# Re-dealing PSUM banks, an earlier store, a ninth buffer and a one-row load in an fp32 attention and mixer kernel

## The chip, the cores and the metric

One core of one Trainium2 chip. The time is the device's time of one execution in microseconds (us), and lower is better. A result is the median of several executions. The profiled execution counts a span that is about 1.8 us shorter than the time; places within the kernel are given on the clock of that span.

## The reference

Two blocks follow each other. The first is a decaying linear attention over 4 x 8 heads, 768 positions and 64 columns, in blocks. The second is a mixer on its output x (4 x 768 x 512): a low-rank mixing along the sequence, and a two-layer product with 2048 hidden columns. Cut to what matters:

```python
Dmask = np.where(rel >= 0, lam[:, None, None] ** rel[None, :, :], 0.0)   # decays, one lam per head
for b in range(nb):                                    # blocks of the sequence
    intra = einsum(einsum(qb, kb) * Dmask, vb)
    inter = einsum(qb * lam_pow, kv_state)
    out[:, :, sl] = intra + inter
    kv_state = lam_block * kv_state + einsum(kb * rev_pow, vb)
x = out.transpose(0, 2, 1, 3).reshape(B, S, H * D)
u = x + (x.transpose(0, 2, 1) @ U @ V).transpose(0, 2, 1)
return u + np.maximum(u @ w_ch1, 0.0) @ w_ch2
```

## The kernel before

Attention goes in 24 steps, one tile of 128 positions in each. Seven steps behind, a tile is mixed (`mix`, giving u) and transposed for the first product (`turn`). Then comes the "head": units of first-product matmuls; among the first three the last mixings and transposes are woven. The rest of the kernel is matmuls back to back. The 8 banks of PSUM are dealt by tag: a ring of four named "bank", and two pairs "pz" and "pd".

```python
x_pool = mix_ctx.enter_context(tc.tile_pool(name="x", bufs=8, side="right"))
consts = att_ctx.enter_context(tc.tile_pool(name="consts", bufs=1))
raw_pool = att_ctx.enter_context(tc.tile_pool(name="raw", bufs=3))     # q, k, v land here
...
def bank(shape, name, tag="bank"):
    return ps.tile(shape, FP32, tag=tag, bufs={"bank": 4}.get(tag, 2), name=name)
lamb = consts.tile([P, H], FP32, name="lamb")
...
# scores: pss -> "pz"; outputs: px -> "pd"; state: pkv -> "pd"
# pq, pk, pxn, pp, pr, pu, put -> "bank"
...
def back(s):
    ...
    xs[s] = x_pool.tile([P, C], FP32, tag="x", name="x_nat")
    nc.scalar.copy(xs[s].rearrange("p (c n) -> p c n", n=P), px)     # copy of x, ScalarE
...
def mix(s):
    pu = bank([P, C], "pu")
    nc.tensor.matmul(out=pu, lhsT=v_hl[:, c * P : (c + 1) * P], rhs=p_hl, start=True, stop=True)
    nc.vector.tensor_tensor(out=xs[s], in0=pu, in1=xs[s], op=ALU.add)   # x becomes u, VectorE
...
def turn(s):
    pt = bank([P, CT, P], "put")
    ...                                            # four transposes of u into put
    if g >= FG:
        ...                                        # ends with uf, ScalarE's copy of put
        nc.sync.dma_start(out=u_d[s], in_=xs.pop(s))
        return
    ...
    def rest():                                    # run in the next step
        ...
        nc.sync.dma_start(out=u_d[s], in_=xs.pop(s))
...
nc.scalar.dma_start(out=lamb, in_=lam.unsqueeze(0).broadcast_to([P, H]))
for name, engine in (("q", nc.sync), ("k", nc.scalar), ("q", nc.sync), ("k", nc.sync), ("v", nc.scalar)):
    load_next(name, engine)
```

In the head and after it, `banks(n, other)` takes pz and pd of a unit from ("bank", "bank") or ("pz", "pd"), in turn.

## Time and profile before

| | before |
|---|---|
| time, median of 3 | 702.17 us (701.72 to 702.33) |
| span of the profiled execution | 700.1 us, granted TensorE clock 1.000 |
| attention, to the last mixing product within it | 145.4 us |
| head, to the last transposes of u | 171.7 us |
| matmuls back to back, to the last one | 695.8 us |

TensorE is the engine that sets the end. So a change of buffers is read in one way: which waits of TensorE go, which come, and at which of these four places. Idle time of another engine matters only where TensorE stands behind it.

### The profile page before, as it was taken

The numbers are of one execution on the slowest core, as the hardware profiler recorded it, in microseconds if no ns is written. First come the engines' busy times: TensorE is split into PE (matmuls) and PEld (weight loads), VectorE is DVE, ScalarE is ACT, GpSimd is POOL, SyncE is SP. The second block draws the span as 40 slices with busy tenths as digits, with TensorE's granted clock in tenths as the row PEclk, the third lists the DMA queues.
The fourth block names the chain that finished last, engine by engine and source line by source line (L and its number), as shares of the span: only waits on it lengthen the run. The fifth ranks groups of instructions, "written<-read, shape, count | busy, mean of one in ns | idle before, by whom it ended". The sixth has DMA issues, their size and how long they took to land.

```text
span 700.1 us, 11380 instructions
## 1 busy us (share of the span) xinstructions
PE 683.6 (98%) x4192; PEld 555.9 (79%) x4192; DVE 501.5 (72%) x903; ACT 305.7 (44%) x543; POOL 108.0 (15%) x91
## 2 busy tenths in 40 slices
PE   6999998998999999999999999999999999999997
PEld 5988787976888888888888888888888888888886
DVE  4777776867899777777779525778676586775864
ACT  3776776855456544444445422232232222322320
POOL 3425444533000000000000000012030030300300
PEclk9999999999999999999999999999999999999999
DMA  9997785414577655556567899956344262353431
GB/s 186 223 204 182 170 202 146 120 47 154 195 258 253 223 195 196 201 203 219 208 210 273 279 320 341 356 201 211 92 155 160 90 211 99 116 191 90 166 92 60
DMA packets 131672, 131.18 MB, mean 187 GB/s; under 512 B 81376, under 2 KB 89568, under 8 KB 131616
## 3 DMA queue, kind: packets, MB, share of 16 engines
q1 hardware_dynamic: 129376, 129.92, 59.0%
q10 hardware_dynamic: 2240, 0.53, 0.4%
q8 instruction: 33, 0.54, 0.3%
q14 instruction: 23, 0.19, 0.1%
HBM read 80.09 MB, written 50.33 MB: 186 GB/s over the span
## 4 chain that ended last, share of the span: by engine, by line
PE 91%; DMA 4%; DVE 3%; ACT 1%; issue 0%; ACTq 0%; DVEq 0%
PE pz L634 25%; PE pz L765 13%; PE pz L767 13%; PE pd L769 13%; PE pd L644 13%; PE pss L343 3%; DMA u_d<-x_nat 3%; PE px L366 2%; PE px L361 2%; PE pxn L406 1%; PE pkv L382 1%; PE put L466 1%; PE pq L308 1%; PE pk L308 1%; DMA kraw<-in_k_dram 1%; DVE sm L349 1%
## 5 line engine op out<-in xcount | busy, mean ns | idle before, releaser
L634 PE MATMUL pz<-u_hl,w 128*128 128x512 f32 x768 | 190.4, 398 | 0.0
L634 PEld LDWEIGHTS pz<-u_hl,w 128*128 128x128 f32 x768 | 144.5, 188 | 35.6 <-issue 0.9
L765 PE MATMUL pz<-w_hl,m 128*128 128x512 f32 x384 | 151.6, 396 | 0.0
L767 PE MATMUL pz<-w_hl,m 128*128 128x512 f32 x384 | 151.6, 396 | 0.0
L769 PE MATMUL pd<-w_d,m 128*128 128x512 f32 x384 | 149.9, 396 | 0.0
L748 ACT ACTIVATE m<-mt 128x512 fp32r<-128x512 f32 x96 | 60.7, 632 | 196.3 <-PE pd L769 146.6
L749 DVE SCALAR_TENSOR_TENSOR m<-rm,m 128x512 fp32r<-128x512 f32 x96 | 71.5, 746 | 55.9 <-ACT m L748 55.5
L649 DVE SCALAR_TENSOR_TENSOR r<-pd,r 128x512 f32<-128x512 f32 x96 | 61.8, 686 | 55.5 <-ACT r L640 42.9
L789 POOL TENSOR_TENSOR o<-o,u 128x512 f32<-128x512 f32 x20 | 29.8, 1524 | 450.7 <-DVE o L787 450.7
L644 PE MATMUL pd<-u_d,w 128*128 128x512 f32 x384 | 98.8, 397 | 0.0
L765 PEld LDWEIGHTS pz<-w_hl,m 128*128 128x128 f32 x384 | 72.3, 188 | 17.7
L769 PEld LDWEIGHTS pd<-w_d,m 128*128 128x128 f32 x384 | 72.3, 188 | 17.7
L767 PEld LDWEIGHTS pz<-w_hl,m 128*128 128x128 f32 x384 | 72.3, 188 | 17.6
L644 PEld LDWEIGHTS pd<-u_d,w 128*128 128x128 f32 x384 | 72.2, 188 | 17.4
L640 ACT ACTIVATE r<-pz 128x512 f32<-128x512 f32 x96 | 51.9, 593 | 71.6 <-PE pz L634 71.6
L750 DVE SCALAR_TENSOR_TENSOR m<-m 128x512 fp32r<-128x512 f32 x96 | 69.1, 721 | 0.9
L747 DVE TENSOR_SCALAR mt<-rm 128x512 uint32<-128x512 uint32 x96 | 46.2, 481 | 24.3 <-DMA rm<-r_d 23.7
L349 DVE TENSOR_TENSOR sm<-pss,mask 128x512 f32<-128x512 f32 x48 | 30.9, 686 | 11.4 <-PE pss L343 9.2
L366 PE MATMUL px<-sm,vraw 128*64 128x128 f32 x384 | 35.5, 274 | 0.0
L179 ACT CAST w<-wt 128x512 fp32r<-128x512 f32 x32 | 19.9, 622 | 31.7 <-DVE wt L176 23.5
L361 PE MATMUL px<-qs,kv 128*64 128x128 f32 x320 | 32.1, 279 | 0.0
L136 ACT ACTIVATE sc<-sc,ends 128x512 f32<-128x512 uint32 x29 | 21.0, 723 | 19.1 <-DVE sc L132 19.1
(84 smaller groups left out, 760.7 us busy)
## 6 DMA issues: line engine op xcount, KB each, us to landing
r_d<-r SPq DMA_DIRECT2D x96, 256.0 KB, 2.9
rm<-r_d SPq DMA_DIRECT2D x96, 256.0 KB, 2.6
words<-in_moe_w_ch_dram SPq DMA_DIRECT2D x32, 512.0 KB, 4.4
w_d<-w SPq DMA_DIRECT2D x16, 768.0 KB, 3.3
w_hl<-w_d SPq DMA_DIRECT2D x16, 512.0 KB, 6.4
u_d<-x_nat SPq DMA_DIRECT2D x24, 256.0 KB, 3.7
u<-u_d SPq DMA_DIRECT2D x24, 256.0 KB, 3.9
out_dram<-o SPq DMA_DIRECT2D x24, 256.0 KB, 2.0
```

What stands on the lines that cost most here:

```text
L366: nc.tensor.matmul(out=px[x * D : (x + 1) * D, a, :], lhsT=vr[:, 2 * a + x, :], rhs=sm[:, x, a, :], start=(c == 0), stop=True,)
L634: nc.tensor.matmul(out=acc[g][0], lhsT=w[:, n, ct, :], rhs=uhl[g][:, n, ct, :], start=(ct == 0 and n == 0), stop=(ct == CT - 1 and n == 1),)
L640: nc.scalar.mul(rs[g], acc[g][0], 1.0 + E)
L644: nc.tensor.matmul(out=acc[g][1], lhsT=w[:, 2, ct, :], rhs=ud[g][:, ct, :], start=(ct == 0), stop=(ct == CT - 1),)
L649: nc.vector.scalar_tensor_tensor(rs[g], acc[g][1], 4096.0, rs[g], ALU.mult, ALU.add)
L747: nc.vector.tensor_scalar(t.bitcast(U32), r.bitcast(U32), HI, None, ALU.bitwise_and)
L748: nc.scalar.activation(out=m[:, 0], in_=t, func=AF.Relu)
L749: nc.vector.scalar_tensor_tensor(m[:, 1], r, 0.0, hi, ALU.max, ALU.subtract)
L750: nc.vector.scalar_tensor_tensor(m[:, 2], hi, E, low, ALU.mult, ALU.subtract)
L765: nc.tensor.matmul(out=pz, lhsT=m[:, 0, cols], rhs=hl[:, 0], start=first, stop=False)
L767: nc.tensor.matmul(out=pz, lhsT=m[:, 1, cols], rhs=hl[:, 1], start=False, stop=end)
L769: nc.tensor.matmul(out=pd, lhsT=m[:, 2, cols], rhs=dd, start=first, stop=end)
```

## The change

The intent is fewer waits of TensorE in attention. Instead of four banks in one ring, each tag has two banks: a1 and a2 take the places of "pz" and "pd", and b1 and b2 those of the ring, with pu moved to a2. The store of u is asked for right behind its transposes, x has nine places, and the results of the first product have four buffers for five, to pay for it. The decays come as one row of 32 bytes and are spread over the 128 partitions by a product with ones; before, a broadcast load read the same 32 bytes 128 times.

```diff
-    x_pool = mix_ctx.enter_context(tc.tile_pool(name="x", bufs=8, side="right"))
+    x_pool = mix_ctx.enter_context(tc.tile_pool(name="x", bufs=9, side="right"))
-    def bank(shape, name, tag="bank"):
-        return ps.tile(shape, FP32, tag=tag, bufs={"bank": 4}.get(tag, 2), name=name)
+    def bank(shape, name, tag):
+        return ps.tile(shape, FP32, tag=tag, bufs=2, name=name)
     def constants():
-        make_identity(nc, ident)
-        make_gather()
-                pt = bank([P, n, P], "p" + name)
+                pt = bank([P, n, P], "p" + name, "b2")
-        pss = [bank([P, HP, P], "pss", "pz") for x in range(2)]
+        pss = [bank([P, HP, P], "pss", "a1") for x in range(2)]
-        px = bank([P, HP, P], "px", "pd")
+        px = bank([P, HP, P], "px", "a2")
-            pkv = bank([P, HP, D], "pkv", "pd")
+            pkv = bank([P, HP, D], "pkv", "a2")
-        px = bank([P, CT, P], "pxn")
+        px = bank([P, CT, P], "pxn", "b1")
-        pp = bank([P, C], "pp")
+        pp = bank([P, C], "pp", "a2" if b < B - 1 else "b2")
-        pr = bank([P, C], "pr")
+        pr = bank([P, C], "pr", "b1" if b < B - 1 else "b2")
-        pu = bank([P, C], "pu")
+        pu = bank([P, C], "pu", "a2" if s < NS - NT - 1 else "b2")
-        pt = bank([P, CT, P], "put")
+        pt = bank([P, CT, P], "put", "b1")
         for ct in range(CT):
             ...                                     # the transposes
+        nc.sync.dma_start(out=u_d[s], in_=xs.pop(s))
         ...
-            nc.sync.dma_start(out=u_d[s], in_=xs.pop(s))      # in both places below
-    nc.scalar.dma_start(out=lamb, in_=lam.unsqueeze(0).broadcast_to([P, H]))
+    lam_row = consts.tile([1, H + P], FP32, name="lam_row")
+    nc.scalar.dma_start(out=lam_row[:, 0:H], in_=lam.unsqueeze(0))
+    nc.vector.memset(lam_row[:, H:], 1.0)
     ...                                             # first loads
+    make_identity(nc, ident)
+    make_gather()
+    pl = bank([P, H], "pl", "a2")
+    nc.tensor.matmul(out=pl, lhsT=lam_row[:, H:], rhs=lam_row[:, 0:H], start=True, stop=True)
+    nc.vector.tensor_copy(out=lamb, in_=pl)
-        r_pool = ctx.enter_context(tc.tile_pool(name="r", bufs=5, reuse_waits="tile"))
+        r_pool = ctx.enter_context(tc.tile_pool(name="r", bufs=4, reuse_waits="tile"))
-        tags = ("bank", "bank") if other else ("pz", "pd")
+        tags = ("b1", "b2") if other else ("a1", "a2")
```

More of the change, by code (lines that the diff above doesn't have):

```diff
@@ L488, in rest @@
             nc.gpsimd.tensor_tensor(out=diff, in0=te, in1=low.bitcast(FP32), op=ALU.subtract)
-            nc.sync.dma_start(out=u_d[s], in_=xs.pop(s))
         turned[s] = rest
```

## The prediction

> **What bounds the kernel now.** I read the page first, then the list of waits, then the chain of work in order of time, then the timeline of three stretches. The page says that TensorE is the engine to watch:
>
> ```profile
> PE 683.6 (98%) x4192; PEld 555.9 (79%) x4192; DVE 501.5 (72%) x903; ACT 305.7 (44%) x543; POOL 108.0 (15%) x91
> ```
>
> With 98% busy no change of buffers can be worth 2% unless the 98% hides slack. It does not, in most of the span. The chain from 173 us on is nothing but matmuls of the two mixer products, back to back:
>
> ```profile
> 173.24 3.75 PE pz L634 x16
> 176.99 1.88 PE pd L644 x8
> ```
>
> 3.75/16 is 0.234 us for each 128x512 matmul. The last one starts at 695.8 us, and 522.5 us / 0.2343 us is 2230, as many as I count between those two times (2231 starts). So from 173 us to 696 us TensorE never waits, and nothing in this change makes a matmul shorter. What is left is the first 173 us (attention with the mixing woven in, then the "head", four units of first-product matmuls among which the last transposes of u lie) and 4 us at the end. In the list of waits of the whole span these lines bear on the change:
>
> ```profile
> ACT x_nat L408 <- DMA u_d<-x_nat: 8.6, 5, 3.4
> ...
> PEld pu L449 <- ACT x_nat L408: 5.1, 4, 2.0
> ...
> PE pu L449 <- ACT x_nat L408: 4.0, 3, 1.8
> ...
> DVE mask L270 <- DMA lamb<-in_lam_dram: 2.3, 1, 2.3
> ```
>
> ScalarE's copy of x (L408) needs one of the eight places for x, and stands until the store of an older u has landed; TensorE's pu (L449) then waits for that copy, because in a ring of four banks its bank is the one of the pxn before. Four times, 5.1 us in all: this is what the change is after. The chain shows one of the four in two lines, the store landing and the copy following it:
>
> ```profile
> 59.02 4.85 DMA u_d<-x_nat
> 63.94 0.59 ACT x_nat L408
> ```
>
> **What the Trainium skill says.** "PSUM — Partial Sum Buffer", section "PSUM bank collisions raise a hardware error", has software guard PSUM by bank: a matmul into a bank waits until the last reader of that bank is done. So the grouping of tags decides who waits for whom; the trace agrees, pu waiting 5.1 us for a copy with which it shares nothing but the bank. "Perfetto Trace Analysis", section "Matmul Optimizations", asks that all 8 banks be in use; both kernels use all 8, so the change only re-deals them. "DMA: Bandwidth & Descriptors", section "Anatomy of one DMA — SWDGE (gpsimd) path", gives about 2 us of fixed cost for a transfer issued on that other path; here the 4 KB broadcast of the decays takes 3.7 us from issue to landing, among large loads, so a transfer of one row may land a little earlier but not for nothing.
>
> **The change, part by part.** In the built kernels every engine has its instructions in the same order up to the end of the head, but for the additions below, the place of the store and a few waits.
>
> 1. *Ninth place for x and an earlier store.* Before, u of tile s-8 was stored in step s, just before x of tile s asked for that place. After, u is stored at the end of the step that adds it, and the place is asked for two steps (2 x 5.6 us) later; a store takes 3.7 us (median), 5.5 at most. The wait goes: -5.1 us on TensorE, as in the list of waits. These are all on the path, since TensorE is.
>
> 2. *Decays as a row.* It adds one matmul of 8 columns, a copy of 128x8 and a memset, and takes away 127 of 128 small descriptors. The scans (2.63 us) now start at 4.43 us and end at 7.06, but the first product with the mask is at 10.35, when the scores are there. TensorE starts at 4.78 on q's load and then waits for k's. The new matmul must be over by 4.78, which a landing like today's 4.4 allows. Gain at most the shorter issue ahead of k on the same queue: -0.2 us.
>
> 3. *r with four places.* The r copy (L640) of a unit then waits for the store of two units before. In the trace of before the smallest distance between such a landing and such a copy is 3.1 us: nothing.
>
> 4. *Banks as four uses of two.* In attention a2 now serves pu, px, pkv in turn: three uses a step in two banks, so pkv takes the bank that pu had in the same step, and must wait until VectorE has added it into x (L452). The built kernel shows this: pkv's first matmul waits for VectorE from step 7 on, where it waited for nothing. One step of before:
>
> ```profile
> 52.23 0.48 PE L449 MATMUL pu<-vp 128*128 128x512 f32 x1
> ...
> 53.73 0.69 DVE L452 TENSOR_TENSOR x_nat<-pu,x_nat 128x512 f32<-128x512 f32 x1
> ...
> 54.33 0.60 PEld L382 LDWEIGHTS pkv<-vraw,ks 128*64 128x64 f32 x16
> 54.44 0.64 PE L382 MATMUL pkv<-vraw,ks 128*64 128x64 f32 x16
> ...
> 55.00 0.97 PEld L343 LDWEIGHTS pss<-qt,kt 64*128 64x128 f32 x16
> ```
>
> The add ends at 54.42 and pkv starts at 54.44: by chance no slack at all. A waiting matmul starts about 0.15 us after the add that it needs:
>
> ```profile
> 161.57 0.68 DVE L452 TENSOR_TENSOR x_nat<-pu,x_nat 128x512 f32<-128x512 f32 x1
> ...
> 162.40 0.63 PE L466 MATMUL put<-ident,x_nat 128*128 128x128 f32 x4 [0.40 <-ACT uf L477]
> ```
>
> (the add ends at 162.25; the copy uf named there ends 0.1 us later, but put reads x.) So pkv is put off by 0.13 us a step, and as VectorE's own work of the step hangs on the scores after pkv, the delay comes anew each time. Step by step, end of the add + 0.15 less pkv's start: step 7 (49.47 against 48.85) 0.77; step 13 (85.50, 85.15) 0.50; step 19 (123.68, 123.59) 0.24; step 22 0.21; eight more at 0.13, 1.04: together 2.8 us. In the steps that TensorE waited out before, pkv had 1 us of room, but that room was the wait. At steps 6, 12 and 18 low's product lies between, in the same two banks: pkv then waits for its copy (step 6: copy ends 42.74, pkv's weights load at 42.54, so 0.25 to 0.3), px for the add (0.1 at 12 and 18), put for low_sum's readers (0.14): about 1.2 us. These delays overlap in part with those of steps 13 and 19, so I take 3.6 us for all.
>
> 5. *The same in the head.* Unit 3 is the first to use b1 and b2. Its two pz alternate from the first matmul on, and both are now in b1, where the last two put are. Before, the ring of four gave the second pz the bank of the last put but one, and the last put's bank went to the second pd, 16 matmuls later.
>
> ```profile
> 171.68 0.63 PE L466 MATMUL put<-ident,x_nat 128*128 128x128 f32 x4 [0.77 <-ACT uf L477]
> ...
> 173.08 1.10 PE L634 MATMUL pz<-u_hl,w 128*128 128x512 f32 x4
> ...
> 173.94 0.59 ACT L477 COPY uf<-put 128x512 f32<-128x512 f32 x1 [0.18 <-DVE u_d L474]
> ```
>
> The last reader of the last put ends at 174.53; the second pz would start at 173.31 and now starts at about 174.65: +1.3 us. In the built kernel the second pz of this unit has the same wait for ScalarE as the first. The products after it rotate as before.
>
> The sum: -5.1 - 0.2 + 3.6 + 1.3 = -0.4 us. From 702.17 that is 701.8 us: the change wins one set of waits and buys another.
>
> **Rivals.** (a) The new bank waits cost nothing, as pkv's weights may be loaded in the shadow of px and VectorE gets ahead once the stores are away. Then -5.3 + 1.3, about 698.2. For it: VectorE is idle some 0.7 us a step, before kvc. Against: that idle time lies after the add, waiting for pkv, so it cannot bring the add forward. (b) The new waits feed on each other: with pkv late, kvc, the kv copies and px of the next step are late as well, or the add falls behind its 128x512 neighbours more often; 0.3 us a step more over 14 steps is +4, about 705. For it: VectorE was busy 17.1 of 20 us from 40 to 60 us. Against: px starts 2.6 us after the scores, and kv's copies end about a microsecond before it. (c) The stores still hide behind the loads, since one queue issues all in order and the DMA engines were 76 to 88% busy in this stretch; the x wait would then stay in part, +1 to +3 on my sum, 703 to 705. Against: two whole steps of room.
>
> **Range and chances.** The gain is measured and bounded by 5.3 us; the loss is my estimate from slacks of a few hundredths of a microsecond, good to perhaps 2 us either way. The executions of before lie within 0.6 us. So 699.0 to 704.2 us. Two per cent are 14 us: the stretch that the change touches has less than that to give back (TensorE's idle time is 16 us in all, with start and end), and a loss of 14 us would need a whole new wait of 0.8 us in each step. Faster 0.01, same 0.98, slower 0.01.
>
> **What would show it.** Right: no wait of the x copy for u's store, no wait of pu for the x copy; a new wait of pkv (its weight load) for the add in most steps from 7 on, 2 to 4 us in all; a step in mid attention of about 5.72 us instead of 5.59; a wait of about 1.3 us of pz for uf where unit 3 begins; matmuls at 0.234 us without a gap after that; attention ending about 1.7 us earlier than before. Wrong: if the pkv waits are missing (rival a) or over 5 us (b), if x copies still wait for stores (c), or if any gap opens after 180 us, where I expect none.

## The result, and the profile after

The changed kernel takes 699.0 us (median of 6, 698.76 to 699.32), against 702.01 us (701.16 to 702.33) for the kernel before in the same rounds: a ratio of 0.9959, with 0.9946 to 0.9972 as the 95% interval. Ratios here are the mean time of one kernel's runs over that of the other's of the same rounds, so not quite the ratio of the medians quoted. The span of the profiled execution went from 700.06 to 697.54 us, with the same granted clock (1.000 and 0.999). The change is worth 2.5 to 3 us: within 2%, but 2.8 us better than I had said.

The first view of the kernel after is the row of busy times on its page: engine, busy us, share, number of instructions.

```profile
PE 685.6 (98%) x4194; PEld 556.0 (80%) x4194; DVE 502.0 (72%) x905; ACT 306.6 (44%) x543; POOL 108.0 (15%) x91
```

It answers to the row of before and says almost nothing: two more matmuls, and the same 98%. The differences have to be read from when TensorE reaches the same instruction in both timelines:

| stretch of TensorE | before, us | after, us | difference | predicted |
|---|---|---|---|---|
| start to the scores of step 1 | 13.18 | 11.80 | -1.38 | -0.2 |
| from there to the 18th pu, the last in attention | 132.18 | 130.05 | -2.13 | -5.1 + 3.6 |
| from there to the last put | 26.32 | 25.94 | -0.38 | 0 |
| from there to the last matmul | 524.09 | 525.45 | +1.36 | +1.3 |
| from there to the end | 4.29 | 4.30 | +0.01 | 0 |

Now the list of waits of the kernel after (engine, tile and line, what it waited for, us in all, times, longest us). No copy of x waits for a store any more, and no pu for the copy of x. In their place stand the waits that the bank tags buy:

```profile
PEld pkv L380 <- DVE x_nat L450: 1.7, 5, 0.7
...
PEld pz L638 <- ACT uf L476: 1.5, 1, 1.5
PEld px L364 <- DVE x_nat L450: 1.4, 2, 0.8
...
PE pz L638 <- ACT uf L476: 1.1, 1, 1.1
```

The timeline of the kernel after (start, duration, engine, line, operation, and in brackets the wait before it) shows two steps of attention, the first where pu's add comes late, the second an ordinary one:

```profile
47.71 0.68 DVE L450 TENSOR_TENSOR x_nat<-pu,x_nat 128x512 f32<-128x512 f32 x1
...
48.44 0.69 PE L380 MATMUL pkv<-vraw,ks 128*64 128x64 f32 x16 [0.50 <-DVE x_nat L450]
...
51.87 0.48 PE L447 MATMUL pu<-vp 128*128 128x512 f32 x1
...
53.38 0.68 DVE L450 TENSOR_TENSOR x_nat<-pu,x_nat 128x512 f32<-128x512 f32 x1
...
54.11 0.69 PE L380 MATMUL pkv<-vraw,ks 128*64 128x64 f32 x16
```

In both, pkv starts 0.05 us after the add ends (48.39 and 54.06): VectorE sets the pace here. Only the first is long enough to be printed as a wait. The list of waits therefore shows less than the tags cost, and the rest is found only by comparing whole stretches. The step from pu to pu is 5.67 us (51.87, 57.54, 63.21), against 5.58 before (46.65, 52.23).

In unit 3 of the head, the timeline of the kernel after has the gap that the prediction gave:

```profile
167.79 0.63 PE L464 MATMUL put<-ident,x_nat 128*128 128x128 f32 x4 [0.41 <-ACT uf L476]
...
169.18 0.40 PE L638 MATMUL pz<-u_hl,w 128*128 128x512 f32 x1
...
170.05 0.59 ACT L476 COPY uf<-put 128x512 f32<-128x512 f32 x1 [0.18 <-DVE u_d L473]
...
170.69 3.78 PE L638 MATMUL pz<-u_hl,w 128*128 128x512 f32 x15 [1.11 <-ACT uf L476]
```

One matmul of pz runs, the second stands until ScalarE has copied the last put out of the bank (170.64), and from there they run on.

What the prediction had not seen is at the start. Timeline of the kernel before:

```profile
4.43 2.63 DVE L270 TENSOR_TENSOR_SCAN mask<-lamb,ident 128x128 f32<-128x128 f32 x8 [2.34 <-DMA lamb<-in_lam_dram]
4.78 0.66 PE L308 MATMUL pq<-ident,qraw 128*128 128x128 f32 x2 [4.78 <-DMA qraw<-in_q_dram]
```

And of the kernel after:

```profile
2.04 0.56 PE L593 MATMUL pl<-lam_row 1*128 1x8 f32 x2 [2.04 <-DMA lam_row<-in_lam_dram]
...
2.84 2.63 DVE L268 TENSOR_TENSOR_SCAN mask<-lamb,ident 128x128 f32<-128x128 f32 x8
...
3.27 0.66 PE L306 MATMUL pq<-ident,qraw 128*128 128x128 f32 x2 [0.67 <-DMA qraw<-in_q_dram]
```

The decays are there at 2.04 us. More to the point, q, which has nothing to do with them, is used at 3.27 us where it was 4.78. Why that is, and where it leads, took half of the experiments.

### The profile page after: what moved, and what is told of

Its sections match the earlier page's. It is cut to its first block, busy times and chain, and to the rows that moved or that the text cites. A ratio compares the mean times of both kernels' runs of the same rounds, so it can differ in the third digit from the quotient of the medians.

```text
span 697.5 us, 11418 instructions
## 1 busy us (share of the span) xinstructions
PE 685.6 (98%) x4194; PEld 556.0 (80%) x4194; DVE 502.0 (72%) x905; ACT 306.6 (44%) x543; POOL 108.0 (15%) x91
## 4 chain that ended last, share of the span: by engine, by line
PE 93%; DVE 4%; issue 1%; ACT 1%; DMA 1%; ACTq 0%; DVEq 0%
PE pz L638 25%; PE pz L771 13%; PE pz L769 13%; PE pd L773 13%; PE pd L648 12%; PE pss L341 3%; PE px L364 3%; PE px L359 2%; PE pxn L404 2%; PE pkv L380 2%; PE put L464 1%; PE pk L306 1%; PE pq L306 1%; DVE ut L469 1%; DVE sm L347 1%; PE pr L433 1%
```

## The experiments

The theory: the gain is the store waits (5 us), the loss is the banks (attention and unit 3), and the start gains because the broadcast hindered the first loads. The rivals: the banks are what helps, as they free pu from the copy of x; the ninth place or the early store does all of it; the start is an accident. Twelve kernels ran, all correct. Times are medians. Each ratio is to the kernel before on the same chip, and different groups ran on different chips.

| run | time, us (range, runs) | before there, us | ratio [95%] |
|---|---|---|---|
| a_row | 697.74 (696.84 to 697.92, 6) | 702.22 | 0.9927 [0.9909, 0.9944] |
| b_store9 | 697.11 (696.44 to 697.41, 6) | 702.22 | 0.9919 [0.9902, 0.9936] |
| c_banks | 703.27 (702.12 to 704.67, 6) | 702.22 | 1.0011 [0.9992, 1.0031] |
| d_no_banks | 694.49 (694.28 to 696.27, 5) | 702.22 | 0.9888 [0.9868, 0.9908] |
| e_store8 | 697.64 (696.80 to 697.76, 5) | 702.42 | 0.9928 [0.9916, 0.9941] |
| f_nine_late | 697.03 (696.59 to 697.39, 4) | 702.42 | 0.9921 [0.9908, 0.9935] |
| g_pz_b2 | 698.02 (697.24 to 699.00, 5) | 702.42 | 0.9937 [0.9923, 0.9951] |
| i_bcast_last | 704.69 (704.19 to 705.60, 5) | 702.42 | 1.0031 [1.0019, 1.0044] |
| h_both | 700.90 (700.83 to 701.76, 5) | 703.42 | 0.9969 [0.9957, 0.9982] |
| k_rows | 700.89 (699.84 to 701.62, 5) | 703.42 | 0.9968 [0.9954, 0.9981] |
| l_late | 700.08 (699.05 to 700.52, 4) | 703.42 | 0.9952 [0.9938, 0.9966] |
| m_pad | 698.27 (697.54 to 699.30, 5) | 701.40 | 0.9953 [0.9939, 0.9966] |

### One part of the change at a time

**b_store9**: the kernel before with the ninth place, the early store and four buffers for r.

```diff
-tile_pool(name="x", bufs=8, side="right")
+tile_pool(name="x", bufs=9, side="right")
+        nc.sync.dma_start(out=u_d[s], in_=xs.pop(s))   # behind the transposes; the two later ones go
-tile_pool(name="r", bufs=5, reuse_waits="tile")
+tile_pool(name="r", bufs=4, reuse_waits="tile")
```

> The kernel before with nine places for x (r with four) and the early store alone. Theory: the four waits of pu for the x copy vanish and nothing takes their place, as the banks stay: 5 us shorter than before (ratio 0.993). Rival: VectorE's loop catches TensorE in the steps that had waited, about 2 us come back: 3 us shorter.

Measured: 5.1 us less. From the scores of step 1 to the 18th pu TensorE took 127.19 us for 132.18, so -4.99, and its list of waits has no line of a copy of x that waits for a store. The first term of the prediction (-5.1) stands to a tenth of a microsecond.

**e_store8** has only the early store, with eight places; **f_nine_late** only the ninth place (and four buffers for r), with the store where it was.

```diff
 # e_store8
+        nc.sync.dma_start(out=u_d[s], in_=xs.pop(s))   # behind the transposes; the two later ones go
 # f_nine_late
-tile_pool(name="x", bufs=8, side="right")
+tile_pool(name="x", bufs=9, side="right")
-tile_pool(name="r", bufs=5, reuse_waits="tile")
+tile_pool(name="r", bufs=4, reuse_waits="tile")
```

> The kernel before with the early store alone, eight places as before. Theory: the store now goes out a step before its place is asked for, some 6 us, and lands in 3 to 5.5 us: the x waits go as with nine places, near 697 us. Rival: the ninth place is what counts, as a landing late by 1 to 2 us still stops the copy: 699 to 700 us.

> The kernel before with nine places (r with four) but the store as late as before. Theory: a place more gives the store a whole step (5.6 us), and no landing was later than 3.5 us past its time: the x waits go, near 697 us, equal to store and place together. Rival: four places for r cost something in the products that the early store hid: 698 us or more, with waits of the r copy for a store.

Measured: 127.25 us in the same stretch for e_store8 (14.35 to 141.60) and 127.19 for f_nine_late (13.44 to 140.63). Each alone takes the whole 5 us, so one of the two parts is redundant. The four buffers for r cost nothing in b_store9 or f_nine_late: the stretch of matmuls stays at 524.09 us.

**c_banks**: the new tags alone.

```diff
-    def bank(shape, name, tag="bank"):
-        return ps.tile(shape, FP32, tag=tag, bufs={"bank": 4}.get(tag, 2), name=name)
+    def bank(shape, name, tag):
+        return ps.tile(shape, FP32, tag=tag, bufs=2, name=name)
# and all tags as in the change
```

> The kernel before with the four uses of two banks alone. Theory: pkv waits for the add in most steps from 7 on and pz for the last put, the x waits stay (they move from pu to a later matmul): 3.5 to 4.5 us longer than before (ratio 1.005 to 1.006). Rival: as pu no longer shares a bank with the x copy, the x wait loses its hold on TensorE and the banks alone pay: 0 to 3 us shorter than before.

Measured: no change that the interval can tell (1.0011). The list of waits of this kernel shows why:

```profile
ACT x_nat L408 <- DMA u_d<-x_nat: 7.7, 5, 2.7
...
PEld pkv L382 <- ACT pt L431: 1.9, 2, 1.0
PEld pkv L382 <- DVE x_nat L452: 1.7, 5, 0.8
...
PEld pz L634 <- ACT uf L477: 1.5, 1, 1.5
```

The copy of x still waits for the store, 7.7 us for 8.6, but pu no longer waits for that copy: it has left the copy's ring. That is what the tags were for, but it is not a gain: 132.13 us in the stretch of attention, as before (132.18), and 525.45 in the last one, +1.36. Of the 5 us in attention, 2.86 are the price of the tags, as in the kernel after (130.05 less 127.19 in b_store9). The other 2.1 are store wait that still reaches TensorE through the queue of ScalarE: step by step against the kernel after, they lie in three steps (0.80, 0.51 and 0.83 us). In two of these pkv stands for pt and in one pxn for xt, and both are copies that ScalarE makes behind the copy of x that stood.

**d_no_banks**: all of the change but the tags; pl takes a bank of "pd".

```diff
 # after, with bank(), its tags and banks() as before
-    pl = bank([P, H], "pl", "a2")
+    pl = bank([P, H], "pl", "pd")
```

> All of the change but the banks. Theory: the parts add, -1.4 for the row and -5 for store and place: 6.5 us shorter than before, near 695.5 us, and 3.5 to 4 us better than the changed kernel; no gap before pkv, none at unit 3 of the head. Rival: the banks are needed for the gain of the ninth place (pu would wait for the pxn copy for another reason): no better than the changed kernel, near 699 us.

Measured: 694.49 us, ratio 0.9888, the fastest of all. Its attention stretch is 127.33 us against 130.05 of the kernel after, and its last stretch 524.09 against 525.45. With the stores out of the way the new tags have nothing left to free, and their price is 2.72 + 1.36 = 4.1 us.

**g_pz_b2**: the kernel after with the two tags of pz and pd swapped where b1 and b2 are used, so that the last two put, in b1, meet pd and not pz.

```diff
-        tags = ("b1", "b2") if other else ("a1", "a2")
+        tags = ("b2", "b1") if other else ("a1", "a2")
```

> The changed kernel with the two tags of the later products exchanged: pz in b2 (where the last pu and low_sum were) and pd in b1 (where the last two put are). Theory: the 1.4 us gap of pz at the start of unit 3 goes, as pd comes 16 matmuls later: 1.3 us shorter than the changed kernel of 699.0, so 697.7 (ratio to before near 0.994). Rival: the gap only moves to pd, or u's split is itself late there (pz needs the split of u): no shorter.

Its timeline at unit 3 is a single line where the kernel after has two with a gap:

```profile
169.23 3.91 PE L638 MATMUL pz<-u_hl,w 128*128 128x512 f32 x16
```

The last stretch is 524.09 us again, and the span 696.22 for 697.54. The gap of unit 3 and its cause are shown: one swapped pair of names takes it away.

### The row of decays, and what came along with it

**a_row**: the kernel before with only the row for the broadcast.

```diff
-    nc.scalar.dma_start(out=lamb, in_=lam.unsqueeze(0).broadcast_to([P, H]))
+    lam_row = consts.tile([1, H + P], FP32, name="lam_row")
+    nc.scalar.dma_start(out=lam_row[:, 0:H], in_=lam.unsqueeze(0))
+    nc.vector.memset(lam_row[:, H:], 1.0)
# and the product with ones, its copy, and the order of make_identity as in the change
```

> The kernel before with the decays as one row alone (banks, places and store as before). Theory: the broadcast of 128 descriptors of 32 bytes holds all first loads back, so the first q transposes start near 3.3 us instead of 4.8 and the whole kernel is 1.3 to 1.5 us shorter than before (ratio 0.998). Rival: the early start of the changed kernel comes from chance in the first transfers or from its other parts; then this run is within 0.3 us of before.

Measured: 4.5 us less, nearly as much as the store's part, and far from the 0.2 us of the prediction. The start gives 1.33 us (scores of step 1 at 11.85), the attention stretch 2.24 (129.94 for 132.18), far away from where the decays are loaded. The list of waits of this kernel tells where:

```profile
ACT x_nat L406 <- DMA u_d<-x_nat: 5.8, 4, 2.5
...
PEld pu L447 <- ACT x_nat L406: 2.8, 4, 1.1
```

The stores of u land sooner (median 3.47 us from issue to landing, 3.83 before, for those issued from 45 to 125 us), so that the wait is 2.8 us where it was 5.1. A load of 32 bytes at 0.7 us cannot do this at 60 us by itself.

**i_bcast_last**: the kernel before with the broadcast issued behind the first loads.

```diff
-    nc.scalar.dma_start(out=lamb, in_=lam.unsqueeze(0).broadcast_to([P, H]))
     for name, engine in (...): load_next(name, engine)
+    nc.scalar.dma_start(out=lamb, in_=lam.unsqueeze(0).broadcast_to([P, H]))
```

> The kernel before, with its broadcast of the decays issued after the first loads of k and v on the same queue instead of ahead of them. Theory: what cost the start was the 128 small reads ahead of the first loads, so q's transposes start near 3.3 us as in the changed kernel and the first scores of step 1 come near 11.8 us, without any row or product: like the row alone, 697.5 to 698.5 us. Rival: it is the number of small descriptors wherever they stand (they then hold back k and v, and the scans get late): within 1 us of before.

Measured: 0.3% slower. The first loads are quicker (scores of step 0 at 6.02 us, 8.24 before), so the broadcast did stand in their way. But the scans now wait 6.5 us for the decays, and the scores of step 1 come at 15.40. The move itself is a loss.

**h_both, k_rows, l_late**: the kernel after with a spare load that nothing reads, so as to bring the suspected cost back: a broadcast of the same 32 bytes right behind the row; 128 different rows of 32 bytes in the same place; the broadcast 30 us later.

```diff
+    spare = consts.tile([P, H], FP32, name="spare")
 # h_both
+    nc.scalar.dma_start(out=spare, in_=lam.unsqueeze(0).broadcast_to([P, H]))
 # k_rows
+    nc.scalar.dma_start(out=spare, in_=q[3, 7, 0:P, 0:H])
 # l_late, in step 6
+            nc.sync.dma_start(out=spare, in_=lam.unsqueeze(0).broadcast_to([P, H]))
```

> The changed kernel with the old broadcast of the decays added again behind the row's load, into a tile that nothing reads. Theory: the broadcast itself is the cost: the first scores of step 1 fall back from 11.8 us to some 13.4, and more than half of the 256-byte packets between 5 and 20 us take over 20 ns again (in all kernels with a broadcast 60 to 80%, in all with the row under 1%); the whole is 1.5 to 2 us longer than the changed kernel, 700.5 to 701 us. Rival: the row's part saves in another way (the scans earlier, TensorE warm earlier), and this run stays near 699 us.

> The changed kernel with another spare load in the same place: 128 pieces of 32 bytes again, but from 128 different rows of q, so nothing is read twice. Theory: reading the same 32 bytes 128 times is what hurts: no slow packets, start as in the changed kernel, 699 us. Rival: the number of small pieces hurts: slow packets and start as with the broadcast, 700.5 to 701 us.

> The changed kernel with the spare broadcast asked for in step 6 (about 37 us) instead of at the start. Theory: the slow packets come with the broadcast and stay for a while after it: under 1% over 20 ns before 35 us and 5 to 20% from 40 to 60 us; time within 1 us of the changed kernel, as loads are ahead by then. Rival: the slow packets need the first loads all started at once by the broadcast: under 1% throughout.

The totals alone would have misled. h_both gave what my theory said, and k_rows gave the number of the rival; the traces support neither reason. The view by stretches has, for each kernel, the stretch, its length, the busy time of TensorE, its weight loads, VectorE, ScalarE and GpSimd, then the granted clock, the DMA share (not capped at 1 here), and GB/s. First the two microseconds in which the broadcast runs and the fifteen after, of the kernel before:

```profile
2.00:4.00 2.00, 0.00 (x0) 0.00 (x0) 0.10 (x2) 0.96 (x1) 0.00 (x0) 1.00 0.52 111
5.00:20.00 15.00, 13.93 (x163) 11.86 (x163) 8.41 (x26) 6.85 (x15) 6.74 (x6) 1.00 1.26 217
```

The kernel after:

```profile
2.00:4.00 2.00, 1.22 (x4) 0.78 (x4) 1.42 (x7) 1.15 (x1) 0.00 (x0) 1.00 0.93 209
5.00:20.00 15.00, 14.96 (x180) 13.13 (x182) 8.11 (x24) 7.90 (x17) 6.87 (x7) 1.00 1.08 248
```

h_both, the broadcast back in place:

```profile
2.00:4.00 2.00, 1.22 (x4) 0.78 (x4) 1.42 (x7) 0.72 (x1) 0.00 (x0) 1.00 0.61 133
```

k_rows, as many pieces from different addresses:

```profile
2.00:4.00 2.00, 1.22 (x4) 0.79 (x4) 1.41 (x7) 0.71 (x1) 0.00 (x0) 1.00 0.87 191
```

l_late, the broadcast not yet issued:

```profile
5.00:20.00 15.00, 14.54 (x163) 12.61 (x164) 7.32 (x21) 6.73 (x15) 6.74 (x6) 1.00 1.12 213
```

From 2 to 4 us the theory holds: the broadcast keeps all loads together at 111 to 133 GB/s, and 128 different rows do not (191, near the 209 without). It is the repeated address, not the number of pieces. What comes behind it is late: in the kernel before and m_pad it is q (used at 4.78 and 4.75 us); in h_both, where the broadcast is issued after the row, q is in time (3.20) but k is not, and the scores of step 0 come at 8.37 us, against 7.45 in k_rows and 7.19 in l_late. But from 5 to 20 us l_late moves only 213 GB/s, as slow as the kernel before, although its broadcast comes 30 us later. So my theory that the broadcast slows the loads after it is refuted. l_late shares something else with the slow ones: its spare tile of 32 bytes.

The tile moves all that is placed behind it. In the built kernels the tiles into which q, k and v land begin 224 bytes past a multiple of 256 in the kernel before, b_store9, c_banks, e_store8, f_nine_late and i_bcast_last, and 32 past one in h_both, k_rows and l_late; both are 32 past a multiple of 64, which is how the text ahead of m_pad below puts it. In the kernel after, a_row, d_no_banks and g_pz_b2 they begin at a multiple of 256, since lam_row takes 544 bytes. I counted, from the records of single DMA packets, those of 256 bytes (the pieces of q, k and v) that take over 20 ns; from 5 to 20 us their median is 24 ns in the kernel before and 18 in the kernel after:

| | 5 to 20 us | 45 to 125 us | store of u, k's load: issue to landing, median us, 45 to 125 us |
|---|---|---|---|
| the nine at 224 or 32 past a multiple of 256 | 39 to 79% | 7.8 to 10.7% | 3.64 to 4.11, 3.84 to 4.13 |
| of these before / l_late | 67% / 39% | 8.7% / 10.7% | 3.83, 3.84 / 4.02, 3.93 |
| after, a_row, d_no_banks, g_pz_b2, at a multiple of 256 | 0.2% | 0.3 to 0.5% | 3.17 to 3.47, 3.41 to 3.59 |

**m_pad** tests just that: the kernel before with an unused tile of 32 bytes, and not one instruction changed. The pad takes q, k and v from 224 past a multiple of 256 to a multiple of 256, so a multiple of 64 or 128 that is none of 256 stays untested.

```diff
     lamb = consts.tile([P, H], FP32, name="lamb")
+    pad = consts.tile([P, H], FP32, name="pad")
```

> The kernel before with one unused tile of 32 bytes a partition among the constants and nothing else: the same instructions, the broadcast too, but all tiles behind it lie 32 bytes further, so that q, k and v land at addresses that are multiples of 64 (as they do, by the size of the new row, in the changed kernel; in the kernel before and in the runs with a spare tile of 32 bytes they lie 32 past one). The run with the late broadcast had its slow 256-byte packets from 5 us on, 30 us before its broadcast, so the broadcast cannot be their cause. Theory now: the address is. Under 1% of the packets take over 20 ns from 5 us on, the x waits shrink from 5.1 to about 3 us, the whole is 2 to 3.5 us shorter than before (699 to 700 us), while the first microseconds stay slow (first q transpose near 4.7 us). Rival: the broadcast does slow the packets as well: over 50% slow between 5 and 20 us, time as before.

Measured: 698.27 us for 701.40, ratio 0.9953 [0.9939, 0.9966]. The slow packets are gone (0.2% and 0.5%). The same view by stretches, with the broadcast still as slow as ever and the loads after it not:

```profile
2.00:4.00 2.00, 0.00 (x0) 0.00 (x0) 0.09 (x2) 0.97 (x1) 0.00 (x0) 1.00 0.53 115
5.00:20.00 15.00, 14.61 (x170) 12.38 (x171) 9.14 (x28) 7.55 (x17) 6.70 (x6) 1.00 1.10 253
```

And its list of waits, to be held against those of before (8.6 and 5.1 us) and of a_row:

```profile
ACT x_nat L409 <- DMA u_d<-x_nat: 6.6, 4, 2.9
...
PEld pu L450 <- ACT x_nat L409: 3.3, 4, 1.5
```

An unused tile goes with 0.72 us less at the start (scores of step 1 at 12.46, within the spread of the start given below) and 1.86 us less in the attention stretch (130.32 us; that stretch is 132.13 to 132.30 in before, c_banks and i_bcast_last). That the pad makes the kernel faster is shown; the way from the packets to the stores is only argued. In attention the loads and the stores go through one DMA queue (q1 of the profile), and both land some 0.35 us sooner (3.48 us for the store, 3.50 for k's load); but in that stretch only 8.7% of the packets of before are slow, and all else that lies behind the pad has moved by 32 bytes too. (x, which is what the stores read, has not: it lies 224 past a multiple of 256 in every kernel.) That is some two thirds of what a_row gained. Two causes are thus told apart: the repeated reads act from 2 to 4 us and on what lands right behind them, the placement wherever q, k and v are loaded. In the changed kernel the second was an accident of the 544 bytes.

How much each is worth at the start can be read only roughly, since kernels of one kind differ there by up to 1.85 us in single profiles. TensorE reaches the scores of step 1 at 12.50 to 14.35 us with neither (five kernels, i_bcast_last left out), at 12.46 with the placement alone, at 13.00 with the row alone (l_late), and at 11.00 to 11.85 with both (four). In times, h_both, k_rows and l_late can't be told from the kernel after (0.9969, 0.9968, 0.9952 against 0.9959, intervals overlapping, other chips): with the store wait gone, the placement has nothing left to win in attention (130.03 to 130.06 us in all four).

## Why the prediction was right or wrong

The range held, but only at its edge: 699.0 us is its lower end, and three of the six executions lie below it. That it held at all is luck. "Within 2%" held for the reason given: the stretch that the change touches has too little to give.

1. **Ninth place and earlier store, -5.1.** Right in size (b_store9: -4.99). That it took both was not claimed, and is not so: either does.
2. **Decays as a row, -0.2.** This is the term that failed. The start gave 1.38 us. The step said "TensorE starts at 4.78 on q's load and then waits for k's", and took the landing of q as given, with only "the shorter issue ahead of k on the same queue" to win. But the loads landed late because the broadcast was running among them: without it, or with it behind the loads, q was used at 3.27 and 3.91 us. The view by stretches of the kernel before had the hint, 111 GB/s from 2 to 4 us against 217 from 5 to 20; I had not asked it for the start. And the size of lam_row moved the landing places of q, k and v, which no step considered.
3. **r with four places, 0.** Right.
4. **Banks in attention, +3.6.** Right in kind, too large in size: 2.7 to 2.9 us (the stretch of 130.05 us less 127.33 in d_no_banks, or 127.19 in b_store9). The assumption that failed is "about 0.15 us after the add". I read that from put, which follows the add by 0.15 us. pkv follows it by 0.05 us. That alone would make about 0.04 us a step; the other 0.05 is in pkv itself, whose sixteen matmuls take 0.69 us where they wait, and 0.64 before. So a step grew from 5.58 to 5.67 us and not to 5.72. In the built kernels the wait of put for the add is an instruction of its own ahead of put, and that of pkv belongs to its first matmul; whether this makes the 0.1 us between them was not tested.
5. **Unit 3, +1.3.** Right: +1.36, in the place and for the copy that I named, and g_pz_b2 takes it away. (The head has six units, with the last transposes in the first three; the prediction wrote four.)

The measured sum is -4.99 + 2.86 - 0.38 + 1.36 - 1.38 = -2.53 us, against -2.52 between the two spans (2.86 is the stretch of the kernel after less that of b_store9). Of the 2.1 us to my -0.4, 1.2 are the start, 0.7 the banks, and 0.4 a stretch of the head where I had put nothing; the first term is 0.1 smaller than I had it. The cause of that 0.38 us stays open: before, the stretch from the 18th pu to the last put takes 26.32 us, and 26.33 in m_pad and 26.32 in i_bcast_last, but 25.94 to 25.97 in all other kernels. It comes with any part of the change, but not with the placement alone. The traces show where it lies: VectorE's first read of the last put but one starts 0.47 us after that put ends in those three kernels (169.51 us in the kernel before), and 0.11 us after it in all others. The profile names pu as the releaser there, but the built kernels wait at this place only for put and for an older product of GpSimd, and both were done.

Of the rivals, (a), no cost of the bank waits, gave 698.2 and came nearer to the time than I did, but for a reason that is not so: the bank waits are there. (b), that they feed on each other, fell: after 2.9 us there is no more. (c), that the stores still hide, fell: no copy of x waits for one.

What the change is worth to this kernel: its tags should not be kept. d_no_banks, the rest without them, is 7.7 us faster than before by the medians, and about 4 us faster than the kernel after by their spans outside the start.

## What to carry to other kernels

Before dealing PSUM banks anew to remove a wait, ask what that wait stands on: here the bank only passed on a late store, and once the store was early the new banks had only their price left. When a part of a change wins more than its own work can explain, and far away from where it acts, compare where the tiles lie: a 32-byte pad won as much as the whole change, and only a kernel that differed in nothing but that pad showed it. A run whose total fits a theory has not confirmed it until its trace shows the mechanism: the times of h_both and k_rows fitted two theories, and l_late's trace refuted the one that I held.

## What the Trainium skill lacked or had wrong

- **Speed of a DMA by the SBUF address it writes to.** "SBUF — State Buffer", section "Operand start alignment", says that DMAs write the right bytes at any element-aligned address, and that this is about legality and its runs timed nothing. "DMA: Bandwidth & Descriptors", section "How a descriptor splits into AXI transactions", says that a transaction reads from a start at a multiple of 256 bytes, and gives no times. Here landing places of 256-byte pieces at 32 or 224 past a multiple of 256 had 39 to 79% of the packets over 20 ns from 5 to 20 us, those at a multiple of 256 had 0.2%, and 32 bytes of padding won 0.47% of the kernel's time. Only these three placements were tried, in this one kind of load. So it is not shown which multiple is needed, nor that the rule of that section is the reason.
- **A broadcast load holds up the others.** No page that I read has it: 128 reads of the same 32 bytes kept the loads together at 111 to 133 GB/s for two microseconds (before, h_both, m_pad), 128 reads of different rows at 191 (k_rows), and without either it was 209.
- **All 8 banks in use is not enough.** "Perfetto Trace Analysis", section "Matmul Optimizations", asks for all 8 banks. Both dealings use all 8, and they differ by 4.1 us (d_no_banks against the kernel after): which tiles share a pair decides.
